# Scale of v in the second attention: one product of bfloat16 row maxima with ones, and the multiplication on ScalarE

## The chip, the cores and the metric

The kernel runs on one core of a Trainium2 chip. The metric is the device time in microseconds (us) of one execution; the figure for a kernel is the median of its runs. The engines are named as in the profile: PE is TensorE, PEld its weight loads, DVE is VectorE, ACT is ScalarE, POOL is GpSimd, SP is SyncE (which here only issues DMAs).

## The reference

Three layers follow each other on 4 batches of 576 rows: a causal attention with decay over 8 heads, a mixing layer with a wide hidden layer of 2048, and a layer of 4 "experts", each of which is a causal attention of its own. Only the last one is touched:

```python
logits = x @ w_gate                      # 4 gate values per row; the two largest are kept
...
for e in range(E):                       # 4 experts
    q = x @ wq[e]; k = x @ wk[e]; v = x @ wv[e]
    scores = scale * (q @ k.transpose(0, 2, 1))
    ...                                  # causal mask, minus the row maximum
    a = np.exp(scores)
    a /= a.sum(-1, keepdims=True) + 1e-09
    ye = a @ v @ wo[e]
    ...                                  # out += gate weight * ye
```

## The kernel before

Single-precision values are carried as a high and a low part and each product is made of three matmuls. For the product of the attention weights with v both are float16 pairs, so v is first brought into float16's range by a power of two.

The second attention is the code from line 900 on. Per batch `b` there are two calls of `experts_qk` (projections to q and k of a pair of experts; each is four pieces of 12 matmuls into a PSUM tile `pq`, whose two halves ACT casts and DVE subtracts, L880 to L892) and one of `expert_values`: five pieces of 12 matmuls into `pv`, copied by ACT to `vr` (L914, 128 partitions x 5 x 260: 256 columns of v and 4 gate values), and then the scale. `value_scale` takes the largest magnitude of each partition on DVE (`am`, L250), has PE turn it into one row (`amt`, L253), reduces that row to one number and cuts it to a power of two (`ar`, L255 to L257), spreads it over the partitions by a product with ones (`rsp`, L262) and takes the reciprocal (`rs`, L264). `value_parts` multiplies v in place on DVE (L269), casts the high part on ACT (`vh`, L270) and has POOL take the low part (`vl`, L271). `gates` then ranks the four gate values and forms the weights `cf`, with twelve small DVE instructions (L836 to L855) and one exponential on ACT (L848). The block `with tc.issue_after(...)` at L928 orders those of its instructions that run on the same engine as the multiplication behind that multiplication.

The loop over the 16 heads (L1038) has one head's scores (`sc`, L212), row maxima of the head after next (`ua` and `ub` on PE, L156 and L169, their masked maxima on DVE, L158 and L176, collected in `mx` and turned by PE into `mt`, L181), and pieces of the work list between them (`work_on`). Exponentials (L221) and casts of them (L222) are on ACT, their low part `pl` (L223) on DVE. In the work list `value_scale` goes in three steps: `am` with the last `pv` piece, then the turning and the `ar` instructions, and two steps later `rsp`, the multiplication, the parts and the gates.

The order on PE is that in which the program is written (`manual_schedule`). The orders of DVE, ACT, POOL and SP come from a planner, which takes what is ready by its own estimate of times and prefers what was written earlier; each engine then works strictly in that order. `amt`, `rsp`, `mt`, `pq`, `pv` and the output products share three PSUM buffers (pool `psf`, tag `f`), so a matmul group that wants a buffer waits until the one three before it has been read. `sc`, `ua` and `ub` share two more (pool `ps2`).

Of the kernel before, what the change touches and what calls it, by code (L numbers as in the profile page):

```python
# [8 lines left out]
F32 = mybir.dt.float32  # L9
F32R = mybir.dt.float32r  # L10
F16 = mybir.dt.float16
BF16 = mybir.dt.bfloat16
I32 = mybir.dt.int32
AF = mybir.ActivationFunctionType
OP = mybir.AluOpType
AX = mybir.AxisListType

P = 128
# [17 lines left out]
PSCALE = 256.0  # L36
VEXP = 8192.0
# [16 lines left out]
def f32(ap):  # L54
    return ap.bitcast(F32)
# [3 lines left out]
def kernel(  # L59
# [13 lines left out]
    nc = tc.nc  # L73
# [4 lines left out]
    def pool(name, bufs=1, side="left", space=None):  # L78
        kw = {} if space is None else {"space": space}
        if space is None:  # L80
            kw["side"] = side
            kw["reuse_waits"] = "tile"
        return tc.alloc_tile_pool(name=name, bufs=bufs, **kw)
# [5 lines left out]
    psf = pool("psf", 3, space=PSUM)  # L89
# [24 lines left out]
    def make_heads(pl_, n, decay):  # L114


        made = []
        for i in range(n):
            qa = pl_.tile([P, S], F32R, name=f"qa{i}")
            qb = pl_.tile([P, S], F32R, name=f"qb{i}")  # L120
            ka = pl_.tile([P, SP_], F32R, name=f"ka{i}")
            kb = pl_.tile([P, SP_], F32R, name=f"kb{i}")
            nc.gpsimd.memset(f32(qa[64:AUG, :]), 1.0)
            nc.gpsimd.memset(f32(ka[:, S:SP_]), 0.0)
            nc.gpsimd.memset(f32(kb[:, S:SP_]), 0.0)
            nc.gpsimd.memset(f32(ka[64:AUG, :S]), -1.0)
            if not decay:
                nc.gpsimd.memset(f32(ka[64:66, :S]), 0.0)
            made.append((qa, qb, ka, kb))
        return made  # L130
# [11 lines left out]
    def drain(gen):  # L142

        while True:
            try:
                next(gen)
            except StopIteration as end:
                return end.value
# [98 lines left out]
    def value_scale(vr):  # L247

        am = small.tile([P, 1], F32, name="am")
        nc.vector.tensor_reduce(am[:], vr, AX.XYZ, OP.max, apply_absolute_value=True)  # L250
        yield
        at_ = psf.tile([1, P], F32, name="amt", tag="f")
        nc.tensor.transpose(at_[:], am[:], ident[:])  # L253
        ar = small.tile([1, 1], F32, name="ar")
        nc.vector.tensor_reduce(ar[:], at_[:], AX.X, OP.max)  # L255
        nc.vector.tensor_scalar(ar[:], ar[:], 1.0e-30, None, OP.max)
        nc.vector.tensor_scalar(ar[:].bitcast(I32), ar[:].bitcast(I32), 0x7F800000, None,  # L257
                                OP.bitwise_and)
        yield

        rp = psf.tile([P, 1], F32, name="rsp", tag="f")
        nc.tensor.matmul(rp[:], ones1[:], ar[:].bitcast(BF16)[:, 1:2], start=True, stop=True)  # L262
        rs = small.tile([P, 1], F32, name="rs")
        nc.vector.reciprocal(rs[:], rp[:])  # L264
        return rs

    def value_parts(vr, rs, vh, vl):

        scaled = nc.vector.tensor_scalar(vr, vr, rs[:, 0:1], VEXP, OP.mult, OP.mult)  # L269
        nc.scalar.copy(vh[:, :, :, 0:64], vr)  # L270
        nc.gpsimd.tensor_tensor(vl[:], vr, vh[:, :, :, 0:64], OP.subtract)  # L271
        return scaled

    def row_scales(av, rs, extra=None):

        den = small.tile([P, NT], F32, name="den")
        nc.vector.tensor_scalar(den[:], av[:, :, 64:65].rearrange("p t o -> p (t o)"),
                                1.0e-9 * PSCALE * VEXP, rs[:, 0:1], OP.add, OP.mult)
        rn = small.tile([P, NT], F32, name="rn")
        nc.vector.reciprocal(rn[:], den[:])  # L280
        if extra is not None:
            nc.vector.tensor_tensor(rn[:], rn[:], extra, OP.mult)
        return rn
# [263 lines left out]
    def attend(p, j):  # L547
        vh, vl = vhs[p % 2]
        ph, pl = st_p[p, j]
        av = weighted_values(ph, pl, vh[:, j], vl[:, j])  # L550
        rn = row_scales(av, st_rs[p])
        normalise(xs[p][:, :, j * D:j * D + D], av, rn)
# [223 lines left out]
    sw = pool("sw")  # L776
# [17 lines left out]
    for k in range(2):  # L794
# [6 lines left out]
    nc.gpsimd.memset(tie[:], 1.0)  # L801
    nc.gpsimd.affine_select(tie[:], tie[:], pattern=[[1, E], [-1, E]], compare_op=OP.is_gt,
                            fill=0.0, base=0, channel_multiplier=0)
    heads = make_heads(hpool, NH2A, False)
    def load_y(b, yp, stp, tag):
        yh = yp.tile([P, KT, SP_], F32R, name="yh", tag="yh")
        yl = yp.tile([P, KT, SP_], F32R, name="yl")
        nc.gpsimd.memset(f32(yh[:, :, S:SP_]), 0.0)
        nc.gpsimd.memset(f32(yl[:, :, S:SP_]), 0.0)
        for c in range(NC):  # L810
            cs = slice(c * HC, c * HC + HC)
            st = stp.tile([P, KT, HC], F32, name="yst", tag=tag)
            nc.sync.dma_start(st[:], ydram[b, :, :, cs])
            for k in range(KT):
                nc.scalar.copy(yh[:, k, cs], st[:, k])
                nc.gpsimd.tensor_tensor(yl[:, k, cs], st[:, k], f32(yh[:, k, cs]), OP.subtract)
        return yh, yl
# [8 lines left out]
    sy = pool("sy", 2, "right")  # L826
# [3 lines left out]
    def gates(lg):  # L830

        a = lg.unsqueeze(2).to_broadcast([P, NT, E, E])
        c = lg.unsqueeze(3).to_broadcast([P, NT, E, E])
        gt = sy.tile([P, NT, E, E], F32, name="gt", bufs=1)
        eq = sy.tile([P, NT, E, E], F32, name="eq", bufs=1)
        nc.vector.tensor_tensor(gt[:], a, c, OP.is_gt)  # L836
        nc.vector.tensor_tensor(eq[:], a, c, OP.is_equal)
        nc.vector.tensor_tensor(eq[:], eq[:], tie[:].unsqueeze(1).to_broadcast([P, NT, E, E]),
                                OP.mult)
        nc.vector.tensor_tensor(gt[:], gt[:], eq[:], OP.add)  # L840
        rank = sy.tile([P, NT, E], F32, name="rank", bufs=1)
        nc.vector.tensor_reduce(rank[:], gt[:], AX.X, OP.add)
        mx = sy.tile([P, NT], F32, name="gmx", bufs=1)
        nc.vector.tensor_reduce(mx[:], lg, AX.X, OP.max)
        ex = sy.tile([P, NT, E], F32, name="gex", bufs=1)
        nc.vector.tensor_tensor(ex[:], lg, mx[:].unsqueeze(2).to_broadcast([P, NT, E]),
                                OP.subtract)
        nc.scalar.activation(ex[:], ex[:], AF.Exp)  # L848
        nc.vector.scalar_tensor_tensor(ex[:], rank[:], 2.0, ex[:], OP.is_lt, OP.mult)
        sm = sy.tile([P, NT], F32, name="gsm", bufs=1)  # L850
        nc.vector.tensor_reduce(sm[:], ex[:], AX.X, OP.add)
        nc.vector.tensor_scalar(sm[:], sm[:], 1.0e-9, None, OP.add)
        nc.vector.reciprocal(sm[:], sm[:])
        cf = sy.tile([P, E, NT], F32, name="cf", bufs=2)
        nc.vector.tensor_tensor(cf[:].rearrange("p e t -> p t e"), ex[:],  # L855
                                sm[:].unsqueeze(2).to_broadcast([P, NT, E]), OP.mult)
        return cf
# [19 lines left out]
    def experts_qk(b, pr, y):  # L877
# [19 lines left out]
        nc.sync.dma_start(f32(kb2[lo_, :S]), f32(tmp[hi_, :]))  # L897
        yield

    def expert_values(b, y):  # L900

        yh, yl = y
        vr = sy.tile([P, NT, NV], F32, name="vr3", bufs=1)
        v0 = 2 * E * D
        for t in range(NT):
            pv = psf.tile([P, 512], F32, name="pv", tag="f")
            ts_ = slice(t * P, t * P + P)
            n = 0
            for k in range(KT):
                for ya, wa in ((yh, wah), (yh, wal), (yl, wah)):  # L910
                    nc.tensor.matmul(pv[:, 0:NV], ya[:, k, ts_], wa[:, k, v0:v0 + NV],  # L911
                                     start=n == 0, stop=n == 3 * KT - 1)
                    n += 1
            nc.scalar.copy(vr[:, t, :], pv[:, 0:NV])  # L914
            if t < NT - 1:
                yield
        vh = sy.tile([P, NT, E, 65], F16, name="vh3")
        vl = sy.tile([P, NT, E, 64], F16, name="vl3")
        nc.gpsimd.memset(vh[:, :, :, 64:65], VEXP)
        vv_ = vr[:, :, 0:E * D].rearrange("p t (e d) -> p t e d", e=E)  # L920
        scale = value_scale(vv_)
        next(scale)
        yield
        next(scale)
        yield
        yield
        rs = drain(scale)
        with tc.issue_after(value_parts(vv_, rs, vh, vl).ins):  # L928
            cf = gates(vr[:, :, E * D:NV])
        st_v[b] = (vh, vl, rs, cf)  # L930
        yield
# [88 lines left out]
    with tc.manual_schedule(engines={mybir.EngineType.PE}):  # L1020
# [7 lines left out]
        work_on(1)  # L1028
        one(m1)
        work.append(expert_values(0, y))  # L1030
        work_on(1)
        one(m1)
# [100 lines left out]
```

## Time and profile before

| what | value |
|---|---|
| time, median of 3 runs | 933.48 us (933.38 to 936.32) |
| the profiled execution's own time | 935.81 us |
| its span in the trace | 934.0 us |
| mean granted clock of PE | 0.958 of full speed |
| second attention (from the last hidden-layer product on) | about 703 to 934 us |

The page of the profile gives shares of the whole span, which holds three different layers. The second attention is therefore read by stretches, with busy time of each engine and the granted clock in each, and then by the waits and the instructions in order of time at the four places where the scale of a batch is formed. Times of rows are microseconds from the start of the span.

### The profile page before, as it was taken

The numbers are of one execution on the slowest core, as the hardware profiler recorded it, in microseconds if no ns is written. First come the engines' busy times: TensorE is split into PE (matmuls) and PEld (weight loads), VectorE is DVE, ScalarE is ACT, GpSimd is POOL, SyncE is SP. The second block draws the span as 40 slices with busy tenths as digits, with TensorE's granted clock in tenths as the row PEclk, the third lists the DMA queues.
The fourth block names the chain that finished last, engine by engine and source line by source line (L and its number), as shares of the span: only waits on it lengthen the run. The fifth ranks groups of instructions, "written<-read, shape, count | busy, mean of one in ns | idle before, by whom it ended". The sixth has DMA issues, their size and how long they took to land.

```text
span 934.0 us, 19003 instructions
## 1 busy us (share of the span) xinstructions
PE 846.4 (91%) x7480; PEld 792.5 (85%) x7480; DVE 562.8 (60%) x1468; ACT 415.9 (45%) x814; POOL 297.2 (32%) x268
## 2 busy tenths in 40 slices
PE   2885898899999989989998999999999897989897
PEld 2774787788899989989998999999999787988685
DVE  6799798687566757532346642222225778786554
ACT  4676665564554454332233332222114554653553
POOL 8456554452523251112144443223024131210100
PEclk9998587999999989999999999999999998999899
DMA  6336465444332342003287652424023221310222
GB/s 191 102 98 171 131 192 152 141 148 138 97 99 74 103 136 73 15 31 98 76 303 259 196 197 88 153 86 122 26 68 98 60 57 26 90 34 20 64 74 80
DMA packets 68777, 101.94 MB, mean 109 GB/s; under 512 B 6608, under 2 KB 49424, under 8 KB 68688
## 3 DMA queue, kind: packets, MB, share of 16 engines
q1 hardware_dynamic: 64416, 92.47, 33.2%
q10 hardware_dynamic: 4272, 8.26, 2.5%
q8 instruction: 59, 0.97, 0.4%
q14 instruction: 30, 0.25, 0.1%
HBM read 60.33 MB, written 22.56 MB: 89 GB/s over the span
## 4 chain that ended last, share of the span: by engine, by line
PE 67%; DVE 15%; DMA 8%; ACT 4%; issue 3%; SPq 1%; POOL 1%; POOLq 0%; ACTq 0%; DVEq 0%
PE cps L387 19%; PE hps L372 18%; PE sc L212 8%; PE pq L868 4%; DVE pl L223 3%; DMA ust<-udram 3%; PE pv L911 3%; PE po L954 2%; DVE ub L176 2%; PE av L239 2%; PE gp L560 2%; PE ub L169 2%; PE av L243 2%; PE av L241 1%; DMA vr<-in_v_dram 1%
## 5 line engine op out<-in xcount | busy, mean ns | idle before, releaser
L387 PE MATMUL cps<-hh,w2h 128*128 128x288 f32 x512 | 156.0, 305 | 5.6 <-DVE yc L389 3.0
L223 DVE TENSOR_TENSOR pl<-pf,ph 128x576 f16<-128x576 f32 x144 | 124.9, 869 | 55.0 <-ACT ph L222 54.8
L387 PE MATMUL cps<-hh,w2l 128*128 128x288 f32 x512 | 152.6, 298 | 1.0 <-POOL w2l L345 1.0
L387 PE MATMUL cps<-hl,w2h 128*128 128x288 f32 x512 | 151.6, 296 | 0.0
L372 PE MATMUL hps<-uh,w1h 128*128 128x288 f32 x512 | 145.6, 305 | 2.8 <-ACT uh L357 2.8
L372 PE MATMUL hps<-uh,w1l 128*128 128x288 f32 x512 | 142.5, 300 | 0.0
L377 DVE SCALAR_TENSOR_TENSOR hl<-hps,hh 128x288 fp32r<-128x288 f32 x128 | 58.2, 455 | 127.5 <-ACT hh L376 127.2
L376 ACT ACTIVATE hh<-hps 128x288 fp32r<-128x288 f32 x128 | 52.3, 409 | 168.8 <-PE hps L372 168.7
L221 ACT ACTIVATE pf<-sc 128x576 f32<-128x576 f32 x144 | 83.6, 612 | 46.6 <-PE sc L212 42.3
L387 PEld LDWEIGHTS cps<-hh,w2h 128*128 128x128 f32 x512 | 97.4, 190 | 7.4 <-DVE yc L389 3.6
L372 PEld LDWEIGHTS hps<-uh,w1h 128*128 128x128 f32 x512 | 98.3, 192 | 3.2 <-ACT uh L357 3.2
L372 PEld LDWEIGHTS hps<-uh,w1l 128*128 128x128 f32 x512 | 98.6, 193 | 0.0
L387 PEld LDWEIGHTS cps<-hh,w2l 128*128 128x128 f32 x512 | 97.1, 190 | 1.2 <-POOL w2l L345 1.2
L387 PEld LDWEIGHTS cps<-hl,w2h 128*128 128x128 f32 x512 | 97.1, 190 | 0.0
L212 PE MATMUL sc<-qa,ka 67*128 67x288 f32 (+4 forms) x288 | 78.3, 332 | 14.9 <-DMA qa<-mr 7.5
L372 PE MATMUL hps<-ul,w1h 128*128 128x288 f32 x512 | 89.1, 296 | 1.8 <-POOL ul L358 1.8
L222 ACT CAST ph<-pf 128x576 f16<-128x576 f32 x144 | 88.8, 638 | 1.5
L239 PE MATMUL av<-vh,ph 128*128 128x65 f16 x720 | 87.8, 204 | 1.5 <-DVE x L286 1.5
L241 PE MATMUL av<-vl,ph 128*128 128x64 f16 x720 | 86.5, 199 | 0.0
L243 PE MATMUL av<-vh,pl 128*128 128x65 f16 x720 | 86.2, 199 | 0.0
L176 DVE CUSTOM_DVE_ANT_0 ub<-ub,maskm 128x448 f32<-128x448 f32 x192 | 81.3, 424 | 6.1 <-PE ub L169 5.0
L358 POOL TENSOR_TENSOR ul<-ust,uh 128x1152 fp32r<-128x1152 f32 x20 | 53.5, 2673 | 79.1 <-ACT uh L357 79.1
(162 smaller groups left out, 1990.7 us busy)
## 6 DMA issues: line engine op xcount, KB each, us to landing
raw<-in_w_dram SPq DMA_DIRECT2D x32, 512.0 KB
ust<-udram SPq DMA_DIRECT2D x22, 576.0 KB
qkt<-in_qk_dram SPq DMA_DIRECT2D x16, 576.0 KB
yc<-ydram SPq DMA_DIRECT2D x14, 576.0 KB
ydram<-yc SPq DMA_DIRECT2D x14, 576.0 KB
vr<-in_v_dram SPq DMA_DIRECT2D x16, 320.0 KB
udram<-ustage ACTq DMA_DIRECT2D x16, 288.0 KB
ydram<-ust SPq DMA_DIRECT2D x8, 576.0 KB
```

What stands on the lines that cost most here:

```text
L176: nc.vector.tensor_tensor_reduce(ub[0:n, bk, off:off + w], ub[0:n, bk, off:off + w], maskm[0:n, m0:m0 + w], 1.0, NEG, OP.add, OP.max, mx[0 ...
L212: nc.tensor.matmul(ps[:, bk, off:off + w], wa, xa, start=bk not in banks[:n], stop=bk not in banks[n + 1:])
L221: nc.scalar.activation(pfv, view, AF.Exp, scale=ISC)
L222: nc.scalar.copy(ph[:, o0:o0 + n], pf[:, 0:n])
L223: nc.vector.tensor_tensor(pl[:, o0:o0 + n], pf[:, 0:n], ph[:, o0:o0 + n], OP.subtract)
L239: nc.tensor.matmul(av[0:m, it, :], ph[0:k, c:c + m], vh[0:k, jt, :], start=first, stop=False)
L241: nc.tensor.matmul(av[0:m, it, 0:64], ph[0:k, c:c + m], vl[0:k, jt, :], start=False, stop=False)
L243: nc.tensor.matmul(av[0:m, it, :], pl[0:k, c:c + m], vh[0:k, jt, :], start=False, stop=last)
L358: nc.gpsimd.tensor_tensor(ul[:], ust[:], f32(uh[:]), OP.subtract)
L372: nc.tensor.matmul(ph[:], wa[:, k, fs], xa[:, k, :], start=n == 0, stop=n == 3 * KT - 1)
L377: nc.vector.scalar_tensor_tensor(hl[:], ph[:], 0.0, f32(hh[:]), OP.max, OP.subtract)
L387: nc.tensor.matmul(pc[:], wa[:, t, dsl], xa[:], start=n == 0, stop=n == 3 * FT - 1)
```

## The change

In the second attention alone the scale is formed otherwise. The maxima of the partitions are written as bfloat16 (`bm`), and one product with a 128 x 128 tile of ones (`every`, set once by POOL) leaves their sum on every partition at once (`bsp`). Three DVE instructions over 128 x 1 divide that by 8192, cut it to a power of two and take the reciprocal (`bs`). The factor 8192, which had been put in with the multiplication, is now in the scale, so the extra column of `vh` that sums the weights holds 1 in place of 8192, and the small constant in `row_scales` loses the factor there. The multiplication of v, in place as before, is an ACT instruction with the scale as an operand of one value per partition. The matmul stands in the step of the work list in which `amt` stood; `rsp` and its step's matmul are gone. The block at the gates now names the ACT multiplication. The first attention keeps `value_scale` and `value_parts`.

```diff
+    every = sw.tile([P, P], BF16, name="every")
+    nc.gpsimd.memset(every[:], 1.0)
...
+    def batch_scale(vr):
+        am = sy.tile([P, 1], BF16, name="bm")
+        nc.vector.tensor_reduce(am[:], vr, AX.XYZ, OP.max, apply_absolute_value=True)
+        yield
+        sp = psf.tile([P, 1], F32, name="bsp", tag="f")
+        nc.tensor.matmul(sp[:], every[:], am[:], start=True, stop=True)
+        rs = sy.tile([P, 1], F32, name="bs", bufs=4)
+        nc.vector.tensor_scalar(rs[:], sp[:], 1.0 / VEXP, 1.0e-30, OP.mult, OP.max)
+        nc.vector.tensor_scalar(rs[:].bitcast(I32), rs[:].bitcast(I32), 0x7F800000, None,
+                                OP.bitwise_and)
+        nc.vector.reciprocal(rs[:], rs[:])
+        yield
+        return rs
+
+    def batch_parts(vr, rs, vh, vl):
+        scaled = nc.scalar.mul(vr, vr, rs[:, 0:1])
+        nc.scalar.copy(vh[:, :, :, 0:64], vr)
+        nc.gpsimd.tensor_tensor(vl[:], vr, vh[:, :, :, 0:64], OP.subtract)
+        return scaled
...
-        nc.gpsimd.memset(vh[:, :, :, 64:65], VEXP)
+        nc.gpsimd.memset(vh[:, :, :, 64:65], 1.0)
...
-        scale = value_scale(vv_)
+        scale = batch_scale(vv_)
...
-        with tc.issue_after(value_parts(vv_, rs, vh, vl).ins):
+        with tc.issue_after(batch_parts(vv_, rs, vh, vl).ins):
             cf = gates(vr[:, :, E * D:NV])
```

In `row_scales` the constant `1.0e-9 * PSCALE * VEXP` becomes `1.0e-9 * PSCALE * (VEXP if extra is None else 1.0)`; `extra` is given by the second attention only.

## Rows read from the trace of the kernel before

**Rows 1.** Page, part 1: busy time, share of the span, instructions of each engine

```profile
PE 846.4 (91%) x7480; PEld 792.5 (85%) x7480; DVE 562.8 (60%) x1468; ACT 415.9 (45%) x814; POOL 297.2 (32%) x268
```

**Rows 2.** Stretches: length, then PE, PEld, DVE, ACT, POOL busy, PE clock, DMA

```profile
727.00:745.00 18.00, 13.92 (x95) 12.93 (x93) 15.84 (x43) 9.58 (x19) 3.30 (x3) 0.91 0.15 33
745.00:765.00 20.00, 20.00 (x226) 19.50 (x224) 14.20 (x40) 12.28 (x30) 6.60 (x8) 1.00 0.31 85
765.00:782.00 17.00, 10.34 (x99) 9.38 (x98) 14.63 (x42) 7.00 (x12) 3.56 (x3) 0.80 0.13 27
...
815.00:832.00 17.00, 12.98 (x135) 12.14 (x135) 14.72 (x44) 8.33 (x16) 2.54 (x1) 0.90 0.10 22
...
848.00:872.00 24.00, 20.91 (x177) 18.45 (x178) 19.36 (x54) 12.96 (x27) 3.07 (x1) 0.89 0.15 32
```

**Rows 3.** Waits from 700 us on: total us, times, longest

```profile
PE amt L253 <- DVE am L250: 5.7, 4, 2.0
...
PE mt L181 <- DVE rn L280: 5.2, 1, 5.2
...
PE mt L181 <- DVE qb L883: 3.1, 1, 3.1
...
PE mt L181 <- DVE rn L282: 2.7, 1, 2.7
...
PE po L954 <- DVE ol L945: 1.8, 1, 1.8
```

**Rows 4.** Groups of DVE instructions from 700 us on: busy us, mean ns | idle before

```profile
L250 DVE TENSOR_REDUCE am<-vr 128x1 f32<-128x1280 f32 x4 | 5.9, 1484 | 2.3 <-ACT vr L914 2.2
L838 DVE TENSOR_TENSOR eq<-eq,tie 128x80 f32<-128x80 f32 x4 | 5.0, 1250 | 0.0
...
L255 DVE TENSOR_REDUCE ar<-amt 1x1 f32<-1x128 f32 x4 | 1.1, 275 | 0.7 <-PE amt L253 0.7
```

**Rows 5.** Groups of ACT instructions from 700 us on, same columns

```profile
L270 ACT CAST vh<-vr 128x1280 f16<-128x1280 f32 x4 | 5.1, 1265 | 4.3 <-DVE vr L269 4.3
```

**Rows 6.** Instructions on tile ar: ns least/median/most, first and last start

```profile
L257 DVE TENSOR_SCALAR ar<-ar x4: 136/142/144, 730.6 to 849.6; 1x1 int32<-1x1 int32 x4
L262 PE MATMUL rsp<-ar,ones x4: 172/172/172, 731.0 to 861.5; 1*128 1x1 bf16 x4
```

**Rows 7.** Second place, in order of time by engine: start, us, instruction, [idle before]

```profile
771.41 1.01 DVE L269 TENSOR_SCALAR vr<-vr,rs 128x1280 f32<-128x1280 f32 x1
...
774.33 2.56 DVE L838 TENSOR_TENSOR eq<-eq,tie 128x80 f32<-128x80 f32 x1
...
777.05 0.13 DVE L176 DVE_READ_ACCUMULATOR2_ANT mx<- 64x1 f32 x1
...
772.46 1.26 ACT L270 CAST vh<-vr 128x1280 f16<-128x1280 f32 x1 [0.62 <-DVE vr L269]
...
773.80 3.00 POOL L271 TENSOR_TENSOR vl<-vr,vh 128x1280 f16<-128x1280 f32 x1 [7.61 <-ACT vh L270]
...
777.24 0.38 PE L181 MATMUL mt<-ident,mx 128*5 128x128 f32 x1 [5.21 <-DVE rn L280]
```

**Rows 8.** First place, the same view

```profile
731.50 1.14 ACT L222 CAST ph<-pf 128x512 f16<-128x512 f32 x2
...
738.64 0.46 DVE L883 TENSOR_TENSOR qb<-pq,qb 64x288 fp32r<-64x288 f32 x1
```

**Rows 9.** Third place, the same view

```profile
821.81 0.22 DVE L838 TENSOR_TENSOR eq<-eq,tie 128x80 f32<-128x80 f32 x1
...
823.12 2.12 DVE L849 SCALAR_TENSOR_TENSOR gex<-rank,gex 128x20 f32<-128x20 f32 x1
```

**Rows 10.** Fourth place, the same view

```profile
867.01 2.32 DVE L840 TENSOR_TENSOR gt<-gt,eq 128x80 f32<-128x80 f32 x1
```

**Rows 11.** Chain that ended last, in order of time: start, us, what

```profile
779.47 2.50 PE pq L868 x12
...
783.26 1.65 PE pq L868 x12
```

More of the change, by code (lines that the diff above doesn't have):

```diff
@@ L277, in row_scales @@
         nc.vector.tensor_scalar(den[:], av[:, :, 64:65].rearrange("p t o -> p (t o)"),
-                                1.0e-9 * PSCALE * VEXP, rs[:, 0:1], OP.add, OP.mult)
+                                1.0e-9 * PSCALE * (VEXP if extra is None else 1.0), rs[:, 0:1], OP.add, OP.mult)
         rn = small.tile([P, NT], F32, name="rn")
```

## The prediction

> **What bounds the kernel now.** I read the page first: PE is busy for 91% of the span, DVE for 60%, ACT for 45% [rows 1]. Over the whole span, then, PE sets the time, and a change to a few DVE and ACT instructions would be worth nothing. The change touches four places only, so the second reading is by stretches. There the picture is another: where a batch's scale is formed PE falls to 13.92 of 18, 10.34 of 17, 12.98 of 17 and 20.91 of 24 us, while DVE is busy for 15.84, 14.63, 14.72 and 19.36 us of them, 81 to 88%. In the stretch between the first two PE is busy for all of its 20 us [rows 2]. The four places cost PE 4.1, 6.7, 4.0 and 3.1 us of idle time, 17.9 us, and the granted clock falls there to 0.80 to 0.91. The third reading is the waits: PE waited 5.7 us in four times for the maxima `am`, once 5.2, once 3.1 and once 2.7 us with the turning `mt` behind DVE work, and 1.8 us with an output product behind DVE [rows 3]. So at these places the bound is DVE's queue, and ACT has room (9.58 of 18, 7.00 of 17, 8.33 of 17 us; 12.96 of 24 at the fourth).
>
> The last reading is the second place in order of time. DVE multiplies v at 771.41 for 1.01 us. At 774.33 one of the gates' small instructions takes 2.56 us and ends at 776.89; its mean over the four is 1250 ns [rows 4], but where it doesn't meet POOL's `vl` it takes 0.22 us [rows 9]; here `vl` runs from 773.80 to 776.80. Behind it in DVE's order stood the last piece of the row maxima; its result is there at 777.18, and PE, idle for 5.21 us, turns it at 777.24 [rows 7]. The releaser that the row names (`rn`) is only what came last before it. The same meeting of a small two-input DVE instruction with `vl` is at each place: 2.12 us at the third, 2.32 us at the fourth [rows 9, 10].
>
> The Trainium skill (SBUF — State Buffer, on engine ports) has a rule for this: VectorE and GpSimd share a pair of ports as an exclusive lock, and a VectorE instruction with two SBUF inputs waits until a GpSimd one that reads SBUF is done. The trace agrees: end of `vl` 776.80, end of the held instruction 776.89.
>
> **The change part by part.**
>
> *DVE.* Per place the multiplication (1.01 us [rows 7]) and the reduction of the row (275 ns [rows 4]) go. The two instructions on `ar` and the reciprocal have three counterparts over 128 x 1; I price all six like the one at L257, 142 ns [rows 6], so they cancel. The maximum keeps its 1484 ns [rows 4]; it writes 128 numbers either way, so its bfloat16 output is taken at nothing. DVE loses 1.29 us per place, 5.1 us in all.
>
> *PE.* One of two small matmuls goes, and the new one stands where `amt` stood and waits for the same maximum, so the 5.7 us of [rows 3] stay. Its price lies between nothing and some 0.2 us beside the `rsp` product's 172 ns [rows 6]; PE is idle there. One fewer PSUM buffer is taken per place. The ones are set once by POOL, where `tie` is set, far ahead of the loop, and nobody waits for them.
>
> *ACT.* It gains the multiplication. The nearest row is the cast of the same 128 x 1280 values, 1265 ns [rows 5]; that is the price I take, with ends of 1.0 us (what DVE needed) and 1.4 us. ACT gets 5.1 us in all, in front of the cast, so the cast and then `vl` follow the scale by 2.5 us where the scale itself no longer waits in DVE's queue. By the Trainium skill (ScalarE: Activation LUTs, What ACT_TABLE_LOAD costs) such an instruction takes 186 + 93 (operand per partition) + 0.833 x 1280, an estimate of 1345 ns; by that ACT would get 0.3 us more in all.
>
> *Gates.* The block orders only what runs on the multiplication's engine. That engine is now ACT, so the gates' DVE instructions no longer queue behind the multiplication; only the exponential does. They read four columns which the multiplication does not write, and `vr` is complete when `am` starts. So they can go into DVE's gaps before `vl` begins, where the two-input ones cost some 0.22 us each [rows 9] and not 2 to 2.5. What follows the exponential (the masked product of L849 first) comes just when `vl` starts, and is then the one that is held; behind it wait DVE's next subtractions and maxima, and for these PE, if it has come to them.
>
> *Sum by place.* Second place: ACT was free at 771.84 (772.46 less 0.62) [rows 7]. With the scale ready by then, multiplication to 773.1, cast to 774.4, `vl` from 774.4. DVE's queue up to `mx` loses 0.95 (multiplication), 0.3 (reduction), 2.34 (2.56 less 0.22 for the held instruction) and gains 0.3 for gates pulled ahead: `mx` at 773.9 in place of 777.2, before the lock is taken. Gain 3.3 us; other end a loss of 0.6, if the gate instruction is held after all, by a `vl` that ends at 777.4. I take 3.3, since its inputs need no scale and are complete before `am` starts.
>
> First place: PE waits for the PSUM buffer that the subtraction at 738.64 sets free. ACT ends its casts at 732.64 [rows 8]; then come, written earlier than the projection's casts and now ready, multiplication and cast, to 735.2. The chain of two ACT casts (0.4 each) and two DVE subtractions (0.46 each) then ends at 737.0, a gain of 2.1 us, or, with the masked product held ahead of it by a `vl` from 735.2 to 738.1, at 739.5, a loss of 0.4. The second is likelier, as the held instruction was written earlier; I take 0.
>
> Third place: the wait of 2.7 us was behind the multiplication and the reduction, with the hold (823.12) after it [rows 3, 9]. Gain 1.2 us; other end 1.0 us of loss, if `vl` starts early enough to hold DVE before `mx`.
>
> Fourth place: the hold at 867.01 stood ahead of what PE waited 1.8 us for [rows 3, 10]. The scale's last step was tied to `rsp` at 861.5, 12 us after `ar` was ready (849.6 [rows 6]); now the scale is ready at about 850, and multiplication, cast, `vl` and gates can go into ACT's and DVE's gaps before 862. Gain 1.8; 0.5 if ACT's multiplication stays there and takes 1.27 back. I take 1.2.
>
> Together 0 + 3.3 + 1.2 + 1.2 = 5.7 us. Behind each place PE runs in its written order and is nearly full, so the gain should reach the end. The profiled execution took 935.81 us, span 934.0 and 1.8 around it, 2.3 above the median of the runs; I take the gain from the median: 933.5 - 5.7 = 927.8.
>
> **The rivals.**
>
> *ScalarE takes the place of VectorE.* Multiplication and cast are 2.5 us in one piece on an engine that works in order, ahead of exponentials and projection casts that PE's buffers wait for. For it: the first place, worked out above; at the fourth ACT has the least room. Against: 7 to 10 us of idle ACT per place [rows 2]. If each place loses the 1.27 us on ACT [rows 5] that it gains on DVE, and one hold is saved (2.3) and one added, 933.5 within 2.5. The same comes out if the gates wait for the multiplication after all, since they read the same tile. The Trainium skill (ScalarE: Activation LUTs, Rules for kernel authors) says to multiply on VectorE, not on ScalarE; the rows, 1.01 and 1.265 us, agree with that, and if both engines stood alike the move would cost 1.0 us in four places.
>
> *Slower: the hold moves in front of PE.* DVE works in order; `vl` holds one instruction at each place for up to 3.00 us [rows 7]. At the third place it came after `mx`; with ACT idle there before the cast, `vl` may start before `mx` is done. Decisive is whether an instruction with two SBUF inputs stands in DVE's order between the start of `vl` and the next result that PE needs. If that is so at the third (2.7 us more, less 1.3) and at the second and first (0.6 and 0.4 more), and ACT costs 1.3 at the fourth: 3.7 us, 937.2.
>
> *More gain: the clock.* After these gaps 12 projection matmuls took 2.50 us, later 1.65 us [rows 11]: the lower clock (1.2 in place of 2.4 GHz for part of them) costs 0.85 us on that piece and, by my estimate from it, as much on the scores ahead of it. If two gaps become short enough that the clock stays, 5.7 + 3.4 gives 924.4; with the first place's 2.1 as well, 922.3.
>
> **How the numbers follow.** Forecast (925 to 930.6) 0.52, ScalarE or gates cancel it (930.7 to 936.2) 0.22, slower (above 936.3) 0.13, clock (below 925) 0.13. A measurement of this kernel can tell about 0.3%, 2.8 us, from no change. So faster is 0.65, same 0.22, slower 0.13. The range leaves out the far ends of the last two: 922.0 to 936.5.
>
> **What the profile after would show.** DVE's busy time from 727 us on down by some 5 us plus saved holds, ACT's up by 5. At the second place `mt` waits less than 3 us, with the gates' rank instructions ahead of `vl` and none of 2 us before `mx`; at the third a wait of 1.5. At the first place the projection's first cast comes behind `vh`, and `mt` waits as long as before. Wrong would be: gate instructions behind the ACT multiplication, a hold ahead of `mx`, PE waiting for ACT casts, or orders of the planned engines so different that PE's losses lie at places which no row above shows.

## The result, and the profile after

| what | before | after |
|---|---|---|
| median of the runs | 933.43 us | 921.86 us |
| ratio, with its 95% interval | | 0.9855 (0.9814 to 0.9896) |
| the profiled execution's own time | 935.81 us | 923.0 us |
| its span in the trace | 934.0 us | 921.2 us |
| second attention, first `pq` matmul to the end of the span | 703.04 to 934.0: 231.0 us | 704.57 to 921.2: 216.6 us |

One of the four executions after was disturbed (1141.17 us): it stands in the median and not in the ratio; the others are 918.0, 920.72 and 923.0. In a second comparison the changed kernel took 923.0 against 932.31 us, 0.9893 (0.9862 to 0.9923). By the medians the change takes off 11.6 us in the first comparison and 9.3 in the second, by the second ratio about 10 us (7 to 13). That is about twice the forecast 5.7, and 921.86 lies 0.14 us below the lower end of the range.

The page, part 1 (busy time, share of the span, instructions of each engine), answers [rows 1]:

```profile
PE 844.2 (92%) x7476; PEld 791.9 (86%) x7476; DVE 552.0 (60%) x1460; ACT 420.5 (46%) x818; POOL 295.6 (32%) x269
```

DVE lost 10.8 us, ACT gained 4.6. The stretches of the second attention, first the whole of it before and then, from the line that begins with 704.57, the whole of it and four stretches after (length, then PE, PEld, DVE, ACT and POOL busy, granted clock, DMA). They answer [rows 2]:

```profile
703.04:934.00 230.96, 202.59 (x1898) 182.83 (x1896) 155.96 (x446) 116.26 (x248) 33.17 (x38) 0.95 0.22 60
```

```profile
704.57:921.20 216.63, 197.10 (x1894) 179.25 (x1892) 146.59 (x438) 120.86 (x252) 31.91 (x38) 0.97 0.24 64
727.00:745.00 18.00, 16.05 (x126) 15.38 (x126) 13.94 (x44) 12.57 (x24) 3.10 (x3) 1.00 0.23 62
765.00:782.00 17.00, 15.00 (x120) 14.30 (x120) 12.96 (x43) 9.40 (x17) 2.54 (x1) 0.70 0.04 9
815.00:832.00 17.00, 14.98 (x136) 14.42 (x137) 14.60 (x45) 9.88 (x19) 2.73 (x2) 0.90 0.11 25
848.00:872.00 24.00, 23.59 (x220) 20.04 (x218) 16.42 (x51) 14.89 (x31) 2.55 (x1) 1.00 0.27 76
```

Of the 14.3 us that the second attention lost, PE's idle time is 8.8 (28.4 to 19.5) and PE's busy time 5.5 (202.59 to 197.10), though it does the same work but for four small matmuls. The busy time goes with the clock (0.95 granted before, 0.97 after): behind some of the waits the same matmuls are slower, as the stretches below show. So there are two gains to be told apart, waits and clock.

The waits after (total us, times, longest), which answer [rows 3]:

```profile
PE bsp L908 <- DVE bm L905: 5.7, 4, 2.0
...
PE mt L181 <- DVE mx L176: 2.2, 2, 2.0
...
PE mt L181 <- DVE gex L851: 1.5, 1, 1.5
...
PE mt L181 <- DVE qb L885: 1.0, 1, 1.0
```

The wait for the maxima is 5.7 us as it was; the three long waits of `mt` were 5.2, 3.1 and 2.7 us and are 1.5, 1.0 and 2.0; the 1.8 us of the output product are gone. The groups of DVE instructions (busy us, mean ns, idle before) answer [rows 4]; the mean says who is held:

```profile
L857 DVE TENSOR_TENSOR cf<-gex,gsm 128x20 f32<-128x20 f32 x4 | 2.9, 715 | 0.1
L854 DVE TENSOR_SCALAR gsm<-gsm 128x5 f32<-128x5 f32 x4 | 2.6, 641 | 0.1
L840 DVE TENSOR_TENSOR eq<-eq,tie 128x80 f32<-128x80 f32 x4 | 0.9, 232 | 0.0
...
L842 DVE TENSOR_TENSOR gt<-gt,eq 128x80 f32<-128x80 f32 x4 | 0.9, 228 | 0.0
```

The rank instructions (L840 and L842 here, L838 and L840 before) are no longer held. An instruction is called held here when it takes clearly longer than usual and ends together with `vl`. Two such holds are left in this profile, on the last instructions of the gates. And on ACT, by tile `bs` (least, median, most ns; first and last start), answering [rows 5, 6]:

```profile
L919 ACT ACTIVATE vr<-vr,bs x4: 1358/1366/1377, 734.0 to 845.3; 128x1280 f32<-128x1280 f32 x4
...
L908 PE MATMUL bsp<-bm,every x4: 163/163/163, 730.4 to 843.7; 128*128 128x1 bf16 x4
```

### The profile page after: what moved, and what is told of

It reads as the page before. It is cut to its first block, busy times and chain, and to the rows that moved or that the text cites. A ratio compares the mean times of both kernels' runs of the same rounds, so it can differ in the third digit from the quotient of the medians.

```text
span 921.2 us, 18992 instructions
## 1 busy us (share of the span) xinstructions
PE 844.2 (92%) x7476; PEld 791.9 (86%) x7476; DVE 552.0 (60%) x1460; ACT 420.5 (46%) x818; POOL 295.6 (32%) x269
## 4 chain that ended last, share of the span: by engine, by line
PE 69%; DVE 12%; DMA 7%; ACT 5%; POOL 4%; issue 3%; SPq 0%; POOLq 0%; ACTq 0%; DVEq 0%
PE cps L387 19%; PE hps L372 18%; PE sc L212 8%; PE pq L870 4%; DMA ust<-udram 3%; PE pv L935 3%; PE po L978 3%; PE av L239 3%; DVE pl L223 3%; PE gp L560 2%; PE ub L169 2%; PE av L243 2%; PE av L241 2%; DVE ub L176 2%; PE ua L156 1%
## 5 line engine op out<-in xcount | busy, mean ns | idle before, releaser
L372 PEld LDWEIGHTS hps<-ul,w1h 128*128 128x128 f32 x512 | 76.9, 191 | 4.6 <-POOL ul L358 3.3
```

The costliest lines, as they stand in the source:

```text
L372: nc.tensor.matmul(ph[:], wa[:, k, fs], xa[:, k, :], start=n == 0, stop=n == 3 * KT - 1)
```

## Where the time went, place by place

Each of the 16 heads has one turning `mt`; its start, counted from the first `pq` matmul, is a milestone that all kernels share. Between the 2nd and the 4th lies the first place, up to the 7th the second, up to the 11th the third, up to the 16th the fourth. Each row of this table is from one profiled execution: by how many us the kernel is ahead of before at that milestone. The last column is from the timed runs.

| kernel | 4th | 7th | 11th | 16th | second attention | ratio to before |
|---|---|---|---|---|---|---|
| before | 0 | 0 | 0 | 0 | 231.0 | |
| after | 4.1 | 6.1 | 6.5 | 14.3 | 216.6 | 0.9855 (0.9814 to 0.9896) |
| after, again | 4.1 | 8.1 | 8.1 | 14.3 | 216.6 | 0.9893 (0.9862 to 0.9923) |
| ones only (e1) | 0.2 | 0.5 | -1.2 | 2.8 | 229.8 | 0.9987 (0.9953 to 1.0021) |
| scale only (e2) | 0.3 | 0.5 | -2.6 | 2.8 | 229.8 | 0.9998 (0.9963 to 1.0034) |
| ScalarE only (e3) | 3.4 | 7.2 | 7.5 | 11.0 | 221.4 | 0.9882 (0.9803 to 0.9961) |
| gates held (e4) | -0.2 | 5.1 | 1.7 | 2.4 | 230.1 | 0.9978 (0.9944 to 1.0012) |
| gates free (e5) | 3.2 | 5.1 | 4.8 | 9.7 | 222.9 | 0.9921 (0.9889 to 0.9954) |
| low part late (e9) | 1.8 | 2.0 | 1.5 | 7.3 | 223.7 | 0.9913 (0.9881 to 0.9945) |
| gates early (e8) | 4.0 | 7.8 | 8.0 | 12.4 | 220.0 | 0.9887 (0.9842 to 0.9931) |

The milestones differ by a few us from one execution to the next, since the clock falls in one and not in the other; e1, in which nothing of the scale is changed, gains 4.0 at the fourth place and gives 1.6 back behind the 16th turning. So a single column says where, and the last says how much.

**First place.** Before, the hold stood here too, ahead of the projection's subtractions that PE waited for; `vl` ran from 734.59 to 737.47:

```profile
735.59 1.98 DVE L838 TENSOR_TENSOR eq<-eq,tie 128x80 f32<-128x80 f32 x1
```

After, in order of time (start, us, engine and instruction, idle before); answers [rows 8]:

```profile
734.02 1.38 ACT L919 ACTIVATE vr<-vr,bs 128x1280 f32<-128x1280 f32 x1
735.29 0.21 ACT L850 ACTIVATE gex<-gex 128x20 f32<-128x20 f32 x1
735.40 0.38 ACT L882 CAST qa<-pq 64x288 fp32r<-64x288 f32 x1
735.68 1.26 ACT L920 CAST vh<-vr 128x1280 f16<-128x1280 f32 x1
```

```profile
735.53 0.18 DVE L851 SCALAR_TENSOR_TENSOR gex<-rank,gex 128x20 f32<-128x20 f32 x1
...
737.02 2.54 POOL L921 TENSOR_TENSOR vl<-vr,vh 128x1280 f16<-128x1280 f32 x1 [8.08 <-ACT vh L920]
...
738.35 0.27 PE L181 MATMUL mt<-ident,mx 128*5 128x128 f32 x1 [1.00 <-DVE qb L885]
```

The planner put the exponential and a projection cast between multiplication and cast. So the masked product of L851 came at 735.53, `vl` only at 737.02, and nothing was held. PE waited 1.00 us, now for ACT's casts, and the clock behind the wait stayed up. The two rows are the stretch from `mt` to the end of the next 12 projection matmuls, before and after:

```profile
739.20:743.50 4.30, 4.26 (x21) 4.02 (x21) 3.77 (x12) 1.72 (x3) 0.00 (x0) 0.64 0.17 37
```

```profile
738.30:741.10 2.80, 2.75 (x21) 2.66 (x22) 2.65 (x7) 1.91 (x4) 1.26 (x1) 1.00 0.51 111
```

The same 21 matmuls take 4.30 us at a granted clock of 0.64 (part at 1.2, part at 2.4 GHz) and 2.80 at 1.00. The place gave 2.4 us at the turning `mt` and 1.5 through the clock, 4.1 with what lies behind.

**Second place**, after; answers [rows 7]:

```profile
771.49 0.13 DVE L176 DVE_READ_ACCUMULATOR2_ANT mx<- 64x1 f32 x1
...
771.67 0.38 PE L181 MATMUL mt<-ident,mx 128*5 128x128 f32 x1 [1.46 <-DVE gex L851]
771.87 2.54 POOL L921 TENSOR_TENSOR vl<-vr,vh 128x1280 f16<-128x1280 f32 x1 [8.26 <-ACT vh L920]
772.37 2.07 DVE L854 TENSOR_SCALAR gsm<-gsm 128x5 f32<-128x5 f32 x1
```

The last row maximum is done before `vl` starts, and the hold (772.37) comes behind it, beside work that PE has. `mt` is 3.0 us ahead of where it would stand with the first place's gain alone. Here the clock gave nothing: PE's 12 projection matmuls behind `mt` ran at 1.2 GHz throughout (granted clock 0.50 from 771.6 to 776.6) and 1.0 us went back, in the second execution nothing. The clock had fallen before this wait: it was 0.72 from 765 to 771, behind the wait of 1.45 us for the maxima.

**Third place**, after; answers [rows 9]. The hold on DVE comes behind the last maximum (816.84):

```profile
817.64 2.54 POOL L921 TENSOR_TENSOR vl<-vr,vh 128x1280 f16<-128x1280 f32 x1 [16.12 <-ACT vh L920]
```

```profile
817.95 2.28 DVE L857 TENSOR_TENSOR cf<-gex,gsm 128x20 f32<-128x20 f32 x1
```

The turning gained 0.8 us, and the stretch from the 7th to the 11th 0.4 in all (in the second execution nothing).

**Fourth place.** Multiplication, cast, `vl` and gates all lie between 843.6 and 851.4, in the gaps as foreseen. Before, PE waited 1.82 us at 870.40 behind the hold [rows 3, 10], and what follows ran at the lower clock. The output products and the matmuls between them, before, after and in e1 (where the wait of 1.8 us is the same):

```profile
870.50:879.50 9.00, 9.00 (x65) 7.26 (x66) 3.60 (x19) 1.76 (x3) 0.00 (x0) 0.64 0.16 58
```

```profile
861.50:867.60 6.10, 6.10 (x67) 4.94 (x65) 2.82 (x13) 1.76 (x3) 0.00 (x0) 1.00 0.23 86
```

```profile
873.50:875.45 1.95, 1.93 (x46) 1.69 (x47) 1.95 (x7) 0.59 (x1) 0.00 (x0) 1.00 0.00 0
875.45:879.75 4.30, 4.30 (x25) 3.38 (x22) 1.68 (x13) 1.18 (x2) 0.00 (x0) 1.00 0.34 122
```

The clock cost 2.9 us in the profiled execution of before. In e1 the wait was there and the clock was full. So of the 7.8 us at the fourth place (6.2 in the second execution) 4.0 come in e1 too, and by this count the change has 2.2 to 3.8. The count is rough, since e6 and e11, which leave the scale alone as well, are 0.8 and 4.9 us ahead there. With 4.1 at the first place, 2.0 to 4.0 at the second and 0 to 0.4 at the third it makes 8.3 to 12.3 us, which agrees with the timed runs; the 14.3 of one pair of profiles is some us too much.

## The experiments

My theory was that the gain comes from the gates' DVE instructions no longer meeting `vl`, since the ordering block now names an ACT instruction; the rivals were the shorter chain of the scale, the load taken from DVE, and an accident of the planner's orders and of addresses.

**e1, ones only.** Before, with only the tile of ones.

```diff
+    every = sw.tile([P, P], BF16, name="every")
+    nc.gpsimd.memset(every[:], 1.0)
```

> The kernel before with nothing but the tile of ones and its one POOL instruction added; nobody reads it. It shifts addresses and may stir the planned orders. If the gain of the change (11.6 us) comes from its named parts, this stays within 1.5 us of 933.4. If orders or addresses that happened to shift make the gain, it moves by several us, to 922 to 930 or above 937.

934.13 against 932.6 us, ratio 0.9987 (0.9953 to 1.0021). In the second attention the orders of all engines in its trace are those of before, so this rules out the addresses; the orders themselves are taken apart in e5 and e9.

**e2, scale only.** After, with the multiplication on DVE, behind which the gates then queue again.

```diff
-        scaled = nc.scalar.mul(vr, vr, rs[:, 0:1])
+        scaled = nc.vector.tensor_scalar(vr, vr, rs[:, 0:1], None, OP.mult)
```

> The new scale (bfloat16 maxima, one product with ones), but the multiplication of v on DVE as before, so the gates' DVE instructions queue behind it as before. Theory A (the gates set free and the multiplication off DVE bring the gain): a gain of the row reduction alone, 0.3 us per place, and at the fourth place the earlier scale: 928 to 933. Theory B (the shorter chain to the scale brings it): 921 to 925.

933.43 us, 0.9998 (0.9963 to 1.0034): no gain that can be told from noise, 0.4 us above theory A's range and far from B's. By places it does change something. The third and the fourth place in order of time:

```profile
820.04 2.55 DVE L840 TENSOR_TENSOR eq<-eq,tie 128x80 f32<-128x80 f32 x1
...
823.25 0.13 DVE L176 DVE_READ_ACCUMULATOR2_ANT mx<- 64x1 f32 x1
...
854.19 2.54 DVE L848 TENSOR_TENSOR gex<-vr,gmx 128x20 f32<-128x20 f32 x1
```

At the third the earlier scale brought `vl` forward and the hold ahead of `mx`; PE's wait for `mt` there grew from 2.7 to 5.3 us, and the place lost 3.1 (e1, without such a hold, 1.7). That is the mechanism of the slower rival, at the place where it was foreseen. At the fourth the hold came 12 us earlier, counted from the first `pq`, beside projection matmuls that PE had to do.

**e3, ScalarE only.** After, with the old scale (the factor 8192 stays out).

```diff
-        scale = batch_scale(vv_)
+        scale = value_scale(vv_)
```

> The old scale (turned maxima, reduction of the row, second product), the multiplication on ACT, the gates free on DVE. Theory A: most of the gain, 922 to 926; it lacks the 0.3 us per place and the early scale at the fourth place, since that still waits for the second product. Theory B: 929 to 934.

927.16 against 932.6 us, 0.9882 (0.9803 to 0.9961), and 11.0 of the 14.3 us at the 16th turning. The median lies between the two ranges, 1.2 us above theory A's, and gives 5.4 us where the ratio gives 11; there were four executions (918.94 to 930.84). The rank instructions take 0.22 us; held are L857 (mean 770 ns) and L854 (711 ns), as in after. Moving the multiplication carries the larger part of the gain; how much of it, four executions don't tell.

**e4, gates held.** After, but with the gates queued behind a DVE copy of one column that reads the multiplied v.

```diff
-        scaled = nc.scalar.mul(vr, vr, rs[:, 0:1])
+        nc.scalar.mul(vr, vr, rs[:, 0:1])
+        mark = sy.tile([P, 1], F32, name="mark")
+        scaled = nc.vector.tensor_copy(mark[:], vr[:, NT - 1, E - 1, 63:64])
```

> The changed kernel, but the gates' DVE instructions queue behind one more DVE instruction (128 x 1) that reads the multiplied v, so they stand behind the multiplication as before. The DVE work taken off (1.3 us per place) stays taken off. If the gates set free are the main cause: 928 to 934, with gate instructions of 2 us or more beside the low part on POOL and PE waiting behind them. If the lighter DVE queue is: 922 to 925.

932.89 us, 0.9978 (0.9944 to 1.0012): scale and multiplication are as in after, and no gain is left that can be told from noise. The groups of DVE instructions have the holds back:

```profile
L842 DVE TENSOR_TENSOR gt<-gt,eq 128x80 f32<-128x80 f32 x4 | 4.9, 1236 | 0.0
...
L840 DVE TENSOR_TENSOR eq<-eq,tie 128x80 f32<-128x80 f32 x4 | 3.1, 766 | 0.0
```

The copy itself waited for ACT 0.2 us in all. The one place that keeps its gain is the second (5.3 us): there the hold (at 775.14, 1.91 us) fell behind the last maximum (771.84). At the first it stood ahead of the projection's subtractions (734.90 for 2.57) and at the third ahead of `mx` (815.67 for 2.37), and these lost. At the fourth no gate instruction was held but the low part `pl` of the exponentials, ahead of the rest of the gates (851.17, 2.64 us in place of 0.76).

**e5, gates free.** Before, without the ordering block; the orders of PE, POOL and SP are those of before.

```diff
-        with tc.issue_after(value_parts(vv_, rs, vh, vl).ins):
-            cf = gates(vr[:, :, E * D:NV])
+        value_parts(vv_, rs, vh, vl)
+        cf = gates(vr[:, :, E * D:NV])
```

> The kernel before with one edit: the gates' instructions are no longer ordered behind the multiplication. Scale, multiplication on DVE, PE, POOL and SP orders stay. If the freed gates alone make the gain: 922 to 926 against 933, the long gate instructions ahead of PE's maxima gone. If the multiplication's 1 us per place on DVE matters as much: half of it, 927 to 930. If freed gates only help once DVE is lighter: 931 to 934.

925.45 against 932.31 us, 0.9921 (0.9889 to 0.9954), 7.4 us by the ratio. DVE still does everything; only its order differs, and on ACT the places of the gates' exponential and a few other instructions. The group of `eq` and the waits for `mt`:

```profile
L838 DVE TENSOR_TENSOR eq<-eq,tie 128x80 f32<-128x80 f32 x4 | 0.9, 220 | 0.0
```

```profile
PE mt L181 <- DVE gsm L851: 3.3, 2, 2.9
...
PE mt L181 <- DVE qb L883: 0.6, 1, 0.6
```

One line, and no new scale, is worth about three quarters of the change (7.4 of 10.0 us on the same chip).

**e9, low part late.** e5 changes two things, the hold and the gates' place in DVE's order. Here the gates stay behind the multiplication, and POOL is made to take the low part behind them.

```diff
-        with tc.issue_after(value_parts(vv_, rs, vh, vl).ins):
+        scaled = nc.vector.tensor_scalar(vv_, vv_, rs[:, 0:1], VEXP, OP.mult, OP.mult)
+        nc.scalar.copy(vh[:, :, :, 0:64], vv_)
+        with tc.issue_after(scaled.ins):
             cf = gates(vr[:, :, E * D:NV])
+        mark = sy.tile([P, 1], F32, name="mark")
+        done = nc.gpsimd.tensor_copy(mark[:], cf[:, 0, 0:1])
+        with tc.issue_after(done.ins):
+            nc.gpsimd.tensor_tensor(vl[:], vv_, vh[:, :, :, 0:64], OP.subtract)
```

> The kernel before; only POOL's low part vl is put behind the gates (behind one 128 x 1 copy on POOL that reads their result). DVE keeps all its work, the multiplication with it, and the gates stay behind the multiplication. If the hold by POOL is what the freed gates avoid: most of their gain, the second attention from 231 to 223 to 226 us. If what counts is where the gates stand in DVE's order, or DVE's load: within 1.5 us of 231.

924.58 against 933.53 us, 0.9913 (0.9881 to 0.9945), 8.1 us. The second place in order of time:

```profile
772.56 1.01 DVE L928 TENSOR_SCALAR vr<-vr,rs 128x1280 f32<-128x1280 f32 x1
...
775.48 0.23 DVE L838 TENSOR_TENSOR eq<-eq,tie 128x80 f32<-128x80 f32 x1
...
775.87 0.13 DVE L176 DVE_READ_ACCUMULATOR2_ANT mx<- 64x1 f32 x1
...
778.17 2.55 POOL L935 TENSOR_TENSOR vl<-vr,vh 128x1280 f16<-128x1280 f32 x1
```

The instruction that took 2.56 us [rows 7] takes 0.23. DVE's work is that of before, and in the second attention so is its order, instruction for instruction; ACT's differs by one copy to `vr` that stands some casts later. So the hold itself is the cause, not DVE's load and not the gates' place in its order. `vl` now holds a `pl` at 779.18 (2.15 us in place of 0.76). This profile is the slowest of the ten executions (930.06): PE's wait for `mt` at the second place is 1.73 us in place of 5.21, but the turning gained only 1.0 us there, as the clock stood at 0.50 from 770 to 776. So the timed ratio, and not the row of the table, says what the hold cost.

**e8, gates early.** After, with the gates written right behind the scale and no block.

```diff
+        cf = gates(vr[:, :, E * D:NV])
         yield
...
-        with tc.issue_after(batch_parts(vv_, rs, vh, vl).ins):
-            cf = gates(vr[:, :, E * D:NV])
+        batch_parts(vv_, rs, vh, vl)
```

> The changed kernel with the gates written right behind the scale, ahead of the multiplication, with no ordering block: their exponential comes before the multiplication on ACT, and all twelve DVE instructions are done before the low part on POOL starts. If what is still held at the second and third place (2.07 and 2.28 us in the changed kernel's trace) costs PE anything: 1 to 3 us less than the changed kernel. If these holds lie beside PE's work: within 1 us of it.

921.33 us, 0.9887 (0.9842 to 0.9931): no gate instruction is held (once a `pl` is, 1.55 us at 767.92). By the medians that is 1.7 us less than after, timed beside it at 923.0, but the intervals overlap, so the two cases can't be told apart. `mt` waits 1.87 and 2.02 us at the second and third place, where after has 1.46 and 2.02: the two holds left in after show no cost there.

**After, again.** On the same chip as e5, e7 and e8.

> The changed kernel once more, beside the other runs of this call on the same chip: 0.985 of the kernel before, with a spread of its runs of some 5 us as in its first timing.

923.0 us, 0.9893 (0.9862 to 0.9923): a smaller gain than the 0.985 expected, with intervals that overlap. The table above has its milestones.

**e6, output tiles.** In before's profile an output copy (ACT, 881.44) waited 2.57 us for a stored row, and in after none does. Before, with three tiles:

```diff
-            ost = sy.tile([P, DM], F32, name="ost")
+            ost = sy.tile([P, DM], F32, name="ost", bufs=3)
```

> The kernel before with three tiles ost in place of two for the output rows, so that ACT's copy doesn't wait for the store of two rows earlier (2.6 us once in the trace before, none in the changed kernel's). If that wait is the part of the fourth place's gain that the forecast did not have: the second attention 2 to 3 us shorter than 231. If it is hidden or comes up elsewhere: within 1 us.

930.6 against 933.53 us, 0.9965 (0.9929 to 1.0000): at the edge of what can be told. That wait is gone and the second attention of the profile takes 230.9 us, as before: it ended on no path that sets the end. The planned orders of DVE and ACT differ in places from those of before, so this is not the wait alone.

**e7, idle matmuls after; e11, the same before.** Six matmuls whose result nobody reads stand ahead of the product with ones (e11: ahead of the turning `amt`), to keep PE busy in its wait for the maxima.

```diff
-        sp = psf.tile([P, 1], F32, name="bsp", tag="f")
+        spw = psf.tile([P, 512], F32, name="bsp", tag="f")
+        for _ in range(6):
+            nc.tensor.matmul(spw[:, 0:448], identb[:], maskm[:, 0:448], start=True, stop=True)
+        sp = spw[:, 0:1]
...
```

> The changed kernel with six idle matmuls (identity times zeros, 448 columns) on PE ahead of the product with ones, where PE waits for the maxima for 1 to 2 us per place; they write the buffer that the product then overwrites. If the lower clock after the second and third place (0.70 and 0.90 granted there) comes from this idle time and its neighbour: 2 to 4 us less than the changed kernel, with clock 1.00 there. If the later wait for mt decides alone: within 1 us of the changed kernel.

> The kernel before with six idle matmuls on PE ahead of the turned maxima, where PE waits for DVE. If the lower clock behind the fourth place (12 projection matmuls in 2.89 us at 850.3 in place of 1.6) comes from that wait: 1 to 2 us less in the second attention, with 1.6 us there. If the clock falls all the same, because of the later and longer waits at the first three places: within 0.5 us of 231.

e7: 920.25 us, 0.9877 (0.9834 to 0.9920), against 923.0 us and 0.9893 of after: 2.8 us less by the medians, but the intervals overlap, and the second attention of its profile takes 216.45 us, as in after. e11: 931.95 us, 0.9998 (0.9969 to 1.0028). Its profile's second attention takes 227.15 us, 3.8 less than before's, with the clock at 1.00 at the fourth place; but e1 has 1.00 there too, without idle matmuls. PE's wait for the maxima falls from 5.7 to 1.3 us in both, and no time that can be told from noise follows. At the fourth place of e7 the clock stayed at 1.00, as in after, but output copies of ACT waited 4.8 us for stored rows.

**e10, both.** e7 with three output tiles and the small tiles of the first attention used again.

> The changed kernel with the six idle matmuls and three tiles ost (the ones then lie in the tile of the first attention's ones, the small tiles in their old places). In the run with idle matmuls alone the fourth place stayed at the full clock, but 4.8 us of waits for stored output rows came up behind it. If those waits took back what the clock gave: the second attention 213 to 215 us, against 216.6 of the changed kernel. If not: 216 to 217.

919.0 against 933.53 us, 0.9846 (0.9788 to 0.9905): not to be told from after. The second attention of its profile takes 216.6 us, the second of the two cases. No version beats the change clearly.

## Where the prediction was right, and which step of it failed

*The mechanism.* The chain holds at each link: the block now binds the gates to ACT, their rank instructions go into DVE's gaps ahead of `vl` (767.32 at the second place), they take 0.23 us, and `mx` is no longer late. e9 shows the hold to be the cause, e5 that freeing the gates is enough for about three quarters of the gain, e4 that without it the rest of the change gives nothing that can be told from noise. What failed is a term of the sum, the first place.

*DVE and ACT.* Multiplication and reduction left DVE as priced: 9.4 us less in the second attention, 5.1 of it the two and the rest holds. The multiplication on ACT took 1.366 us where I took 1.265, 0.4 in all, inside the ends of 1.0 and 1.4. The Trainium skill's price (ScalarE: Activation LUTs, What ACT_TABLE_LOAD costs), which I set beside the sum at 1.345, was the nearer one; what the multiplication took beyond the cast is 101 ns, where the Trainium skill gives 93 there for the operand per partition. Its rule to multiply on VectorE (the Trainium skill, same page, Rules for kernel authors) would have kept the block on DVE and the gain away; e2 is that kernel.

*PE.* The wait for the maxima stayed at 5.7 us, and `bsp` costs 163 ns in an idle PE. Right.

*First place: forecast 0, measured 4.1.* This is the step that failed. I worked out both ends (2.1 gained, 0.4 lost), held the second for likelier, as "the held instruction was written earlier", and took 0. That took multiplication and cast as one piece of 2.5 us on ACT, with the gates' exponential behind it, so that the masked product would meet `vl`. The planner put the exponential and a projection cast between the two; the masked product came 1.5 us ahead of `vl`, and the last of the gates started at 736.87, 0.15 us before it. So the 1.98 us hold of before went and none came in its place. The turning came 2.4 us earlier, and the clock, 0.64 before, stayed at 1.00. The second execution gives the same 4.1, and in e1 the place moves by 0.2. It is the larger part of what the sum lacks: 5.7 was forecast, the places make 8.3 to 12.3.

*Second place: forecast 3.3, measured 3.0* at `mt`. Right in size and mechanism.

*Third place: forecast 1.2, measured 0.8.* `mt` still waits 2.0 us there, for the maxima themselves, where 1.5 was forecast.

*Fourth place: forecast 1.2, measured 2.2 to 3.8* beyond what e1 has. The 1.8 us wait is gone, as reckoned; not in the sum was the lower clock behind it, 2.9 us in that execution and none in e1.

*The clock* was a rival with a chance of 0.13 and a price of 0.85 us a piece. "If two gaps become short enough": one surely did (first place), the second did not (0.50 after, with a wait of 1.46 us in place of 5.21), and at the fourth it comes and goes without the change. With the first place's 2.1 it gave 922.3, and that is near what came, in part by luck: of its two gaps only one is shown to have kept the clock. The two terms were weighed one by one; at the first place they went together, since the clock stayed where the wait became short.

*The rivals.* That ScalarE takes DVE's place came true at the first place alone, where PE now waits for casts, 1.00 us in place of 3.14. The slower rival did not come in the change, but its mechanism exists: it is e2's third place.

*Not settled.* Between e3 and after lie 3.3 us at the 16th turning, between e5 and after 4.6, of profiles that differ among themselves by as much; the timed ratios of the three overlap. What the earlier scale adds to free gates is not shown.

## What to carry to other kernels

Where a small instruction of an engine takes ten times its usual duration, look for what runs on the other engine at that moment, and ask which instruction that PE needs stands behind it in the same queue: reordering a few instructions, or the long one, was worth about three quarters of this change. An ordering rule that names an instruction changes its meaning when that instruction moves to another engine. Price a wait of PE with the matmuls behind it, which may run at half the clock (0.50 at the second place).

## What the runs showed of the hardware

`vl` on POOL holds more than what reads two tiles of SBUF: the one-input L854 over 128 x 5 took 2.07 us at 772.37 beside `vl` and 0.17 alone (847.20). Not everything is held: the reciprocal L855 over the same 128 x 5 took its 0.19 us beside `vl` (817.72), and so did subtractions with one input in PSUM (`qb`, 0.45 us at 737.27). The Trainium skill (SBUF — State Buffer, SBUF: two separate sides) names for the lock, besides instructions with two SBUF inputs, those in a two-port mode; I had carried over only the instructions with two inputs. The trace agrees if L854 runs in such a mode, which no run shows by itself.

The same order of PE's work, with the same wait of 1.8 us ahead, ran at a granted clock of 0.64 in one execution and of 1.00 in another (before and e1), 2.9 us apart in some 65 matmuls. And what lies behind the 16th turning took 31.3 us in before and 32.9 in e1, with all engines in the same order; the clock in the last 9 us was 1.00 in the one and 0.69 in the other. What decides between the two is not shown.
